# Grouping weight products into two runs instead of three, with row sums in the output bank, in an attention + ReGLU kernel on one core

## Chip, cores, metric

One core of one Trainium2 chip. The metric is device time in microseconds (us) of one execution. Executions of one kernel in one series lie 0.2 to 2.1 us apart; each kernel is told with the median and the lowest and highest of its fast runs (no timed run was in the slow state; single executions have no state).

## The reference, cut to what matters

```python
# x [8, 8, 512, 64], state [8, 8, 32, 64]: batches, heads, rows, width
a  = softmax(x @ state.T / 8);  xread = a @ state
a2 = softmax(state @ x.T / 8);  sread = a2 @ x
y  = concat([xread, sread])              # per batch 512 + 32 rows, 8 heads x 64 = 512 columns
out = (relu(y @ w_gate) * (y @ w_val)) @ w_out     # 512 -> 1536 -> 512
```

## The kernel before

The kernel never forms `xread`. Per batch it multiplies the small state by the gate and value weights ("weight products", `up`, kept in `U`, bf16), and then `gv` multiplies `U` by the normalised scores. `gv` goes in 12 slices of 128 columns of the 1536; after each slice TensorE (PE) runs a piece of an earlier batch's output product (`out_piece`). One thing more is hung into certain slices: scores, weight products, and row sums (`sr`) for the second softmax. These are the parts that matter:

```python
def bank(name, kind="r"):            # PSUM has 8 banks: 0 to 5 rotate, 6 and 7 are for output pieces
    ...
    n = turn["r"] % 6 if kind == "r" else 6 + turn["o"] % 2
    turn[kind] += 1
...
def u_unit(b, w, lo):                # one weight-product unit: 8 matmuls of 64x32 tiles, 512 columns
    ps = held["u", b, w, lo] = [bank("up"), bank("up")]        # two banks
    u_mm(ps, b, w, lo, 512)
...
def u_block(b, lo, engs=("act", "act", "dve", "dve")):         # a run: two units, four casts out of PSUM
    for w in range(2):
        u_unit(b, w, lo)
        for kc in range(NK):
            u_out(b, w, lo, kc, engs[2 * w + kc])

def att_half(b, kc):                 # scores, exp (ScalarE), then sums and scaling on VectorE
    att_up(b, kc)
    ...
first, lag = 2 * NF + 4, 18
at(2, 4, x_dma, 4, (nc.sync,))
for b in range(3, B):
    s, late = b - 1, 2 if b == 3 else 0        # batch b's work is hung into the slices of batch b-1
    for i, jf in enumerate((3, 5)):
        at(s, jf + late, att_half, b, i)
    for i, jf in enumerate((7, 9, 11)):
        at(s, jf, u_block, b, 512 * i)
    ...
for g in range(first, NF * (B + 1)):
    b, jf = divmod(g, NF)
    gv(b, jf) if b < B else gvs(jf)
    relu(b, jf)                      # ScalarE, reads the first bank of gv
    mult(b, jf)                      # VectorE: h = value * relu(gate), reads the second bank
    if g >= lag:
        out_piece(*divmod(g - lag, NF))
    for f in units.get(g, ()):       # what was hung in with at(...)
        f()
```

Each engine runs its instructions in the order in which the program emits them. "Batch 2's slices" are those of `gv(2, ...)`; batch 3's scores and weight products are in them. The scheduled part that is discussed starts at slice 4 of batch 2; a hand-made program before it is the same in both kernels.

The softmax here doesn't subtract the row's maximum and nothing guards it: scores larger than these inputs give would overflow.

Of the kernel before, what the change touches and what calls it, by code (L numbers as in the profile page):

```python
# [16 lines left out]
def kernel(  # L17
# [9 lines left out]
    nc = tc.nc  # L27

    B, H, S, D = x.shape
# [5 lines left out]
    NF = d_ff // 128  # L35
# [19 lines left out]
    NK = 2  # L55
# [7 lines left out]
    NX, DP = 2, 66  # L63
# [15 lines left out]
    given, turn = [], {"r": 0, "o": 0}  # L79

    def bank(name, kind="r"):

        if given:
            n = given.pop(0)
        else:
            n = turn["r"] % 6 if kind == "r" else 6 + turn["o"] % 2
            turn[kind] += 1
        return psum.tile([128, 512], FP32, name=name, tag=f"b{n}")

    held = {}  # L90
# [33 lines left out]
    def state_T(g):  # L124
        ps = held["st", g] = bank("stT_ps").bitcast(BF16)[:, 0:512]
        for i in range(4):
            nc.tensor.transpose(ps.rearrange("p (q i m) -> p q i m", i=4, m=8)[:, :, i],
                                st_b[:, g % 3, i].rearrange("p h d -> p (h d)"), id128)
# [31 lines left out]
    def x_T(b, j):  # L160

        if b not in xT:
            xT_alloc(b)
        ps = bank("xT_ps").bitcast(BF16)[:, 0:512].rearrange("p (c t) -> p c t", c=NC)
        for c in range(NC):
            if b == 0 and j < 2:
                nc.tensor.transpose(ps[:, c], x_head(b)[:, c, 2 * j:2 * j + 2].rearrange("p h d -> p (h d)"), id128)
            else:
                v, h = (x_tail(b), 2 * j - HK) if b == 0 else (xb[b], 2 * j)
                for h2 in range(2):  # L170
                    nc.tensor.transpose(ps[64 * h2:64 * h2 + 64, c], v[:, c, h + h2], id128)
        held["xT", b, j] = ps
# [4 lines left out]
    def x_T2(b, half):  # L177
        if b not in xT:
            xT_alloc(b)
        ps = held["xT2", b, half] = bank("xT_ps").bitcast(BF16).rearrange("p (c j t) -> p c j t", c=NC, j=2)  # L180
        for j in range(2):
            for c in range(NC):
                for h2 in range(2):
                    nc.tensor.transpose(ps[64 * h2:64 * h2 + 64, c, j], xb[b][:, c, 4 * half + 2 * j + h2], id128)  # L184
# [68 lines left out]
            src = src.rearrange("p c h d -> p h c d")  # L253
            nc.gpsimd.tensor_copy(out=v[:, hs:hs + src.shape[1]], in_=src)  # L254

    def sr_mm(b):

        ps = held["sr", b] = bank("sr_ps")[:, 0:2 * DP].rearrange("p (r d) -> p r d", r=2)
        for c in range(NC):
            for parity in range(2):  # L260
                for j in range(NJ):
                    nc.tensor.matmul(ps[32 * j:32 * j + 32, parity, 0:D + 1], e_sn[b][:, parity, c, 32 * j:32 * j + 32],  # L262
                                     xa[:, b % NX, H * c + 2 * j + parity, 0:D + 1],
                                     start=(c == 0 and parity == 0), stop=(c == NC - 1), skip_group_check=True)

    def sr_norm(b):
        ps = held["sr", b]
        rr = small.tile([128, 2], FP32, name="rr", tag="rr")
        nc.vector.reciprocal(out=rr, in_=ps[:, :, D])
        sn = held["sn", b] = small.tile([128, 2, D], BF16, name="sn", tag="sn")  # L270
        nc.vector.tensor_tensor(out=sn, in0=ps[:, :, 0:D], in1=rr.to_broadcast([128, 2, D]), op=ALU.mult)
# [20 lines left out]
    def u_unit(b, w, lo):  # L292

        u_alloc(b)
        ps = held["u", b, w, lo] = [bank("up"), bank("up")]
        u_mm(ps, b, w, lo, 512)

    def u_out(b, w, lo, kc, eng):
        copy[eng](out=U[b][:, w, kc, lo:lo + 512], in_=held["u", b, w, lo][kc])  # L299
# [17 lines left out]
    def gv(b, jf):  # L317
        if b not in hsb:
            hsb[b] = hpool.tile([128, NF, S], BF16, name="h_sb", tag="h_sb")
        held["gv", b, jf] = [bank("gv_ps"), bank("gv_ps")], hsb[b][:, jf], S  # L320
        for w in range(2):
            for kc in range(NK):
                gv_mm(held["gv", b, jf][0], b, jf, w, kc)

    def gvs(jf):
        f0 = jf * 128
        ps = [bank("gv_ps"), bank("gv_ps")]
        nt = B * Ns
        for w, wsb in ((0, wg_sb), (1, wv_sb)):
            for j in range(NJ):  # L330
                nc.tensor.matmul(ps[w][:, 0:nt], wsb[:, j, f0:f0 + 128], br[:, j].rearrange("p b n -> p (b n)"),  # L331
                                 start=(j == 0), stop=(j == NJ - 1))
        held["gv", B, jf] = ps, hs_sb[:, jf], nt

    def relu(b, jf):
        ps, dst, n = held["gv", b, jf]
        g_sb = held["g", b, jf] = gpool.tile([128, 512], BF16, name="g_sb", tag="g_sb")
        nc.scalar.activation(out=g_sb[:, 0:n], in_=ps[0][:, 0:n], func=AF.Relu)  # L338

    def mult(b, jf):  # L340
        ps, dst, n = held["gv", b, jf]
        nc.vector.tensor_tensor(out=dst, in0=ps[1][:, 0:n], in1=held["g", b, jf][:, 0:n], op=ALU.mult)  # L342
# [4 lines left out]
    def out_mms(src, b, tsub, jfs):  # L347
        if jfs[0] == 0:
            held["o", b, tsub] = o_bank()
        for jf in jfs:  # L350
            nc.tensor.matmul(held["o", b, tsub], src[:, jf, tsub * 128:(tsub + 1) * 128], wo_sb[:, jf],  # L351
                             start=(jf == 0), stop=(jf == NF - 1))
# [4 lines left out]
    def fin_x(b, tsub, eng="act"):  # L357
        o_sb = opool.tile([128, d_model], FP32, name="o_sb", tag="o_sb")
        copy[eng](out=o_sb, in_=held["o", b, tsub])  # L359
        nc.sync.dma_start(out=out_rows(b, tsub), in_=o_sb)  # L360

    def fin_s(t2):
        outr = out.rearrange("(b s) m -> b s m", s=SP)
        o_sb = opool.tile([128, d_model], FP32, name="o_sb", tag="o_sb")
        nc.scalar.copy(out=o_sb, in_=held["o", B, t2])
        for bq in range(4):
            eng = nc.sync if bq % 2 == 0 else nc.scalar
            eng.dma_start(out=outr[t2 * 4 + bq, S:SP], in_=o_sb[bq * Ns:(bq + 1) * Ns])
# [14 lines left out]
    def out_part(b, i):  # L383
        tsub, q = divmod(i, 3)
        out_mms(hsb[b], b, tsub, list(range(4 * q, 4 * q + 4)))

    def out_piece(b, i):
        out_part(b, i)
        if i % 3 == 2:
            fin_x(b, i // 3)  # L390
# [37 lines left out]
    def spin(n, cols=512):  # L428
        for i in range(n):
# [6 lines left out]
             "sc": att_sc, "ex": att_exp, "nr": att_sum, "nx": att_scale, "aT2": att_T2, "ao2": att_out2, "aT": att_T, "ao": att_out,  # L436
             "c": c_unit, "co": c_out, "u": u_unit, "uo": u_out, "gv": gv, "re": relu, "mu": mult, "o": out_part,
             "of": fin_x, "xn": x_next, "xp": x_pad, "sr": sr_mm, "sn": sr_norm}
    program = """
    dx.1.0.2 dx.1.1.2 stc.0.0.act stc.0.1.dve spin.7 stT.0@0 xc.0.0.dve dw.0.0.128 sto.0.act dw.1.0.128 on xc.0.1.dve  # L440
# [31 lines left out]
        assert not given  # L472


    units = {}

    def at(b, jf, f, *args):
        units.setdefault(NF * b + jf, []).append(lambda: f(*args))

    def u_block(b, lo, engs=("act", "act", "dve", "dve")):  # L480
        for w in range(2):
            u_unit(b, w, lo)
            for kc in range(NK):
                u_out(b, w, lo, kc, engs[2 * w + kc])

    def att_half(b, kc):
        att_up(b, kc)
# [7 lines left out]
        att_scale(b, kc)  # L495

    def sr(b):
        sr_mm(b)
        sr_norm(b)

    def state_prep(lo, hi):
# [2 lines left out]
            state_out(g, "act")  # L504

    first, lag = 2 * NF + 4, 18
    at(2, 4, x_dma, 4, (nc.sync,))
    at(2, 10, state_prep, 4, B)
    for b in range(3, B):
        s, late = b - 1, 2 if b == 3 else 0  # L510
        for i, jf in enumerate((3, 5)):
            at(s, jf + late, att_half, b, i)
        for i, jf in enumerate((7, 9, 11)):
            at(s, jf, u_block, b, 512 * i)
        if b + 1 < B:
            at(s, 9, x_next, b + 1)
            at(s, 9, x_pad, b + 1)
        if b + 2 < B:
            at(s, 10, x_dma, b + 2, (nc.sync,))
    for b in range(B):  # L520
        s, jf = {0: (2, 2), 1: (2, 3), 2: (2, 8), 3: (2, 11)}.get(b, (b - 1, 9))
        if b > 1:
            at(s, jf, sr, b)
        at(*divmod(NF * s + jf + 2, NF), sr_T, b, "act")
    for g in range(first, NF * (B + 1)):
        b, jf = divmod(g, NF)
        gv(b, jf) if b < B else gvs(jf)
        relu(b, jf)
        mult(b, jf)
        if g >= lag:  # L530
            out_piece(*divmod(g - lag, NF))
        for f in units.get(g, ()):
            f()
    for t2 in range(2):
        out_mms(hs_sb, B, t2, list(range(NF)))
        fin_s(t2)
# [33 lines left out]
```

## Time and profile before

226.34 us (226.18 to 226.71, 3 runs); the profiled execution spans 224.4 us.

| | before |
|---|---|
| PE busy | 98% |
| VectorE / ScalarE / GpSimd busy | 57% / 56% / 24% |
| chain of waits that ended last | 91% PE |
| gv slice or output piece | 0.865 us, start to start |
| a batch in the steady part | 23.76 us |

From the page of the kernel before: the busy table, the clock granted to PE by slice (tenths), and the chain of waits by engine.

```profile
PE 219.3 (98%) x1967; PEld 104.8 (47%) x1967; DVE 128.6 (57%) x226; ACT 124.8 (56%) x236; POOL 53.0 (24%) x58
...
PEclk9999999999999999999999999999999999999999
...
PE 91%; DMA 4%; POOL 3%; issue 0%; DVE 0%; POOLq 0%; DVEq 0%
```

PE has almost no time off, so the busy share says nothing about where it loses. For that the timeline of PE is better read by differences of starts. The columns are start, time taken, engine, line, operation, output and inputs, tile, shape and count; matmuls overlap, so the times taken add to more than the time that passes. This is the kernel before in batch 4's slices 7 to 11 and on:

```profile
111.17 1.03 PE L351 MATMUL o_ps<-wo_sb,h_sb 128*128 128x512 bf16 x4
112.13 0.41 PE L289 MATMUL up<-wg_sb,stT 64*32 64x512 bf16 x8
112.36 0.40 PE L289 MATMUL up<-wv_sb,stT 64*32 64x512 bf16 x8
112.69 1.04 PE L314 MATMUL gv_ps<-ans,U 128*128 128x512 bf16 x4
...
120.95 0.40 PE L289 MATMUL up<-wv_sb,stT 64*32 64x512 bf16 x8
121.28 0.23 PE L275 MATMUL srT_ps<-id,sn 128*128 128x128 bf16 x1
121.35 1.20 PE L314 MATMUL gv_ps<-ans,U 128*128 128x512 bf16 x4
122.38 1.02 PE L351 MATMUL o_ps<-wo_sb,h_sb 128*128 128x512 bf16 x4
```

The piece at 111.17 has the array for 0.865 us, to 112.035. The first unit starts at 112.13, 0.095 late; the second 0.23 later; `gv` follows the second by 0.33 where a further unit would follow by 0.23. So this run pays about 0.10 us to enter and 0.10 to leave. Units use the array in tiles of 64x32, `gv` and the pieces use it whole (128*128 in the lines); entering and leaving are changes of that mode. At 121.35 `gv` holds the array until 122.38, 1.03 us instead of 0.865.

### The profile page before, as it was taken

How to read it: one execution, taken by the hardware profiler on the slowest of the kernel's cores; microseconds unless marked ns; L12 is line 12 of the kernel's file. 1: busy time of each engine (PE TensorE's matmuls, PEld its weight loads, DVE VectorE, ACT ScalarE, POOL GpSimd, SP SyncE). 2: the span in 40 equal slices, each digit the busy share in tenths (PEclk: the TensorE clock that was granted, in tenths of full speed). 3: DMA queues.
4: the chain of work that ended last, by engine and by line, in shares of the span. 5: the costliest groups of instructions: out<-in, count | busy, mean ns of one | idle time of the engine just before them, and what ended most of it. 6: DMA issues, size and time to landing. Idle time of an engine off the chain costs nothing.

```text
span 224.4 us, 4871 instructions
## 1 busy us (share of the span) xinstructions
PE 219.3 (98%) x1967; PEld 104.8 (47%) x1967; DVE 128.6 (57%) x226; ACT 124.8 (56%) x236; POOL 53.0 (24%) x58
## 2 busy tenths in 40 slices
PE   7999999999999999999999999999999999999994
PEld 3544454444444444434444443445444445666543
DVE  3687788576486667754866477646865433222100
ACT  4699877773666655664466455655546444322221
POOL 8798756412352150015000600000000000000000
PEclk9999999999999999999999999999999999999999
DMA  6999999160809612681159213511311111112132
GB/s 155 177 195 197 209 231 282 41 167 0 250 34 197 227 48 80 144 246 51 48 124 261 84 47 78 112 50 47 93 50 47 48 47 50 48 58 75 58 94 93
DMA packets 37799, 25.48 MB, mean 114 GB/s; under 512 B 18864, under 2 KB 33200, under 8 KB 37776
## 3 DMA queue, kind: packets, MB, share of 16 engines
q1 hardware_dynamic: 24912, 16.85, 26.6%
q0 software_dynamic: 11968, 7.47, 21.5%
q10 hardware_dynamic: 896, 0.85, 1.3%
q8 instruction: 15, 0.25, 0.5%
q14 instruction: 8, 0.07, 0.1%
HBM read 18.35 MB, written 8.91 MB: 121 GB/s over the span
## 4 chain that ended last, share of the span: by engine, by line
PE 91%; DMA 4%; POOL 3%; issue 0%; DVE 0%; POOLq 0%; DVEq 0%
PE o_ps L351 38%; PE gv_ps L314 37%; PE gv_ps L331 5%; PE up L289 4%; DMA wv_sb<-in_moe_w_val_dram 4%; PE upc L289 1%; PE sr_ps L262 1%; PE sc_ps L198 1%; PE o_ps L377 1%; POOL wg_sb L108 1%; POOL xb L418 1%; POOL wv_sb L108 1%; PE xT_ps L184 0%; PE aT_ps L233 0%; POOL xb L410 0%; PE srT_ps L275 0%
## 5 line engine op out<-in xcount | busy, mean ns | idle before, releaser
L314 PE MATMUL gv_ps<-ans,U 128*128 128x512 bf16 x384 | 96.7, 380 | 0.1
L351 PE MATMUL o_ps<-wo_sb,h_sb 128*128 128x512 bf16 x372 | 94.6, 379 | 0.0
L338 ACT ACTIVATE g_sb<-gv_ps 128x512 bf16<-128x512 f32 (+1 forms) x108 | 63.1, 584 | 47.0 <-PE gv_ps L314 32.5
L342 DVE TENSOR_TENSOR h_sb<-gv_ps,g_sb 128x512 bf16<-128x512 f32 x96 | 65.3, 688 | 41.8 <-ACT g_sb L338 40.5
L351 PEld LDWEIGHTS <-h_sb 128*128 128x128 bf16 x372 | 36.0, 98 | 41.0 <-issue 0.7
L314 PEld LDWEIGHTS <-U 128*128 128x128 bf16 x384 | 34.8, 98 | 41.4 <-issue 4.2
L359 ACT COPY o_sb<-o_ps 128x512 f32<-128x512 f32 x29 | 17.0, 585 | 20.7 <-PE o_ps L351 20.7
L299 DVE CAST U<-up 128x512 bf16<-128x512 f32 x36 | 23.2, 685 | 5.3 <-PE up L289 5.2
L299 ACT CAST U<-up 128x512 bf16<-128x512 f32 x36 | 19.4, 592 | 10.1 <-PE up L289 10.1
L140 POOL CAST xb<-xf 128x1024 bf16<-128x1024 f32 x10 | 10.4, 1066 | 53.2 <-DMA xf<-in_x_dram 53.2
L254 POOL COPY xa<-xb 128x2048 bf16<-128x2048 bf16 (+1 forms) x9 | 15.3, 1710 | 13.8 <-issue 7.0
L211 DVE TENSOR_REDUCE cs<-e_sn 128x16 f32<-128x512 bf16 x16 | 10.9, 684 | 8.6 <-ACT e_sn L205 8.6
L342 DVE TENSOR_TENSOR hs_sb<-gv_ps,g_sb 128x256 bf16<-128x256 f32 x12 | 5.1, 425 | 15.4 <-PE gv_ps L331 10.5
L205 ACT ACTIVATE e_sn<-sc_ps 128x512 bf16<-128x512 f32 x16 | 9.6, 600 | 5.6 <-PE sc_ps L198 5.5
L309 ACT CAST U<-upc 128x512 bf16<-128x512 f32 (+1 forms) x20 | 9.7, 532 | 1.4 <-PE upc L289 1.3
L289 PEld LDWEIGHTS <-stT 64*32 64x32 bf16 x512 | 5.0, 89 | 11.2 <-issue 10.9
L430 PE MATMUL warm_ps<-hs_sb 128*128 128x512 bf16 x23 | 7.8, 456 | 1.2 <-DVE hs_sb L394 1.2
L217 DVE TENSOR_TENSOR a_sn<-e_sn,rc 128x512 bf16<-128x512 bf16 x12 | 8.3, 692 | 0.6
L198 PEld LDWEIGHTS <-xT 128*128 128x128 bf16 x128 | 5.7, 98 | 3.8 <-ACT xT L175 0.7
L331 PE MATMUL gv_ps<-br,wg_sb 128*128 128x256 bf16 x48 | 7.2, 273 | 0.0
L331 PE MATMUL gv_ps<-br,wv_sb 128*128 128x256 bf16 x48 | 7.2, 273 | 0.0
L289 PE MATMUL up<-wg_sb,stT 64*32 64x512 bf16 x144 | 7.2, 386 | 0.0
(64 smaller groups left out, 129.0 us busy)
## 6 DMA issues: line engine op xcount, KB each, us to landing
out_dram<-o_sb SPq DMA_DIRECT2D x31, 256.0 KB, 2.3
xf<-in_x_dram SPq DMA_DIRECT2D x4, 1024.0 KB, 6.5
wo_sb<-in_moe_w_out_dram POOLq DMA_DIRECT2D x2, 768.0 KB, 14.5
wg_sb<-in_moe_w_gate_dram POOLq DMA_DIRECT2D x5, 256.0 KB, 8.8
wv_sb<-in_moe_w_val_dram POOLq DMA_DIRECT2D x5, 256.0 KB, 9.4
xf<-in_x_dram POOLq DMA_DIRECT2D x1, 1024.0 KB, 15.2
xb<-in_x_dram POOLq DMA_DIRECT2D x3, 256.0 KB, 6.3
xb<-in_x_dram POOLq DMA_DIRECT2D x1, 512.0 KB, 11.6
```

What stands on the lines that cost most here:

```text
L140: copy[eng](out=xb[b][:, :, hs].rearrange("p c h d -> p h c d"), in_=xf[b][:, hs])
L211: nc.vector.reduce_sum(out=cs, in_=e_v, axis=AX.X)
L254: nc.gpsimd.tensor_copy(out=v[:, hs:hs + src.shape[1]], in_=src)
L289: nc.tensor.matmul(dst[parity][32 * j:32 * j + 32], stT[r:r + 64, b, j, 32 * parity:32 * parity + 32], wsb[r:r + 64, j, lo:lo + n], start= ...
L299: copy[eng](out=U[b][:, w, kc, lo:lo + 512], in_=held["u", b, w, lo][kc])
L309: copy[eng](out=U[b][:, :, kc, lo:lo + n], in_=held["c", b, lo][kc])
L314: nc.tensor.matmul(ps[w], U[b][:, w, kc, f0:f0 + 128], ANS[b][:, kc].rearrange("p c t -> p (c t)"), start=(kc == 0), stop=(kc == NK - 1))
L331: nc.tensor.matmul(ps[w][:, 0:nt], wsb[:, j, f0:f0 + 128], br[:, j].rearrange("p b n -> p (b n)"), start=(j == 0), stop=(j == NJ - 1))
L338: nc.scalar.activation(out=g_sb[:, 0:n], in_=ps[0][:, 0:n], func=AF.Relu)
L342: nc.vector.tensor_tensor(out=dst, in0=ps[1][:, 0:n], in1=held["g", b, jf][:, 0:n], op=ALU.mult)
L351: nc.tensor.matmul(held["o", b, tsub], src[:, jf, tsub * 128:(tsub + 1) * 128], wo_sb[:, jf], start=(jf == 0), stop=(jf == NF - 1))
L359: copy[eng](out=o_sb, in_=held["o", b, tsub])
```

## The change

Three things. The six units of a batch form two runs of three units (slices 7 and 10) instead of three runs of two. Three units take all six rotating banks, so the next output piece is run early, right behind the run, to give ScalarE and VectorE time to empty banks. And the row sums take the output bank that is idle at that time. Around it, batch 3's scores move from slices 5 and 7 to 4 and 6, batch 4's load from slice 4 to 6, the preparation of the later states (`state_prep`) from 10 to 8, row sums of batches 2 and 3 to slices 7 and 10 and later ones to 10, and later transposes to one slice behind their sums.

```diff
+        elif kind == "spare":
+            n = 6 + turn["o"] % 2
...
-    def u_block(b, lo, engs=("act", "act", "dve", "dve")):
-        for w in range(2):
+    def u_block(b, part):
+        for w, lo in ((0, 0), (1, 0), (0, 512), (1, 512), (0, 1024), (1, 1024))[3 * part:3 * part + 3]:
             u_unit(b, w, lo)
-            for kc in range(NK):
-                u_out(b, w, lo, kc, engs[2 * w + kc])
+            u_out(b, w, lo, 0, "act")
+            u_out(b, w, lo, 1, "dve")
...
     def sr(b):
-        sr_mm(b)
+        sr_mm(b, "spare")
...
-    at(2, 4, x_dma, 4, (nc.sync,))
-    at(2, 10, state_prep, 4, B)
+    at(2, 6, x_dma, 4, (nc.sync,))
+    at(2, 8, state_prep, 4, B)
     for b in range(3, B):
-        s, late = b - 1, 2 if b == 3 else 0
+        s, late = b - 1, 1 if b == 3 else 0
         for i, jf in enumerate((3, 5)):
             at(s, jf + late, att_half, b, i)
-        for i, jf in enumerate((7, 9, 11)):
-            at(s, jf, u_block, b, 512 * i)
+        for part, jf in enumerate((7, 10)):
+            at(s, jf, u_block, b, part)
+            paired.add(NF * s + jf)
...
-        s, jf = {0: (2, 2), 1: (2, 3), 2: (2, 8), 3: (2, 11)}.get(b, (b - 1, 9))
+        s, jf = {0: (2, 3), 1: (2, 4), 2: (2, 7), 3: (2, 10)}.get(b, (b - 1, 10))
...
-        at(*divmod(NF * s + jf + 2, NF), sr_T, b, "act")
+        at(s, jf + (2 if b in (2, 3) else 1), sr_T, b, "act")
...
         for f in units.get(g, ()):
             f()
+        if g in paired:
+            out_piece(*divmod(piece, NF))
+            piece += 1
```

More of the change, by code (lines that the diff above doesn't have):

```diff
@@ L254, in x_pad, with sr_mm @@
             nc.gpsimd.tensor_copy(out=v[:, hs:hs + src.shape[1]], in_=src)
-    def sr_mm(b):
-        ps = held["sr", b] = bank("sr_ps")[:, 0:2 * DP].rearrange("p (r d) -> p r d", r=2)
+    def sr_mm(b, kind="r"):
+        ps = held["sr", b] = bank("sr_ps", kind)[:, 0:2 * DP].rearrange("p (r d) -> p r d", r=2)
         for c in range(NC):
@@ L472 @@
         assert not given
-    units = {}
+    units, paired = {}, set()
     def at(b, jf, f, *args):
         units.setdefault(NF * b + jf, []).append(lambda: f(*args))
-    def u_block(b, lo, engs=("act", "act", "dve", "dve")):
-        for w in range(2):
+    def u_block(b, part):
+        for w, lo in ((0, 0), (1, 0), (0, 512), (1, 512), (0, 1024), (1, 1024))[3 * part:3 * part + 3]:
             u_unit(b, w, lo)
-            for kc in range(NK):
-                u_out(b, w, lo, kc, engs[2 * w + kc])
+            u_out(b, w, lo, 0, "act")
+            u_out(b, w, lo, 1, "dve")
     def att_half(b, kc):
@@ L520 @@
     for b in range(B):
-        s, jf = {0: (2, 2), 1: (2, 3), 2: (2, 8), 3: (2, 11)}.get(b, (b - 1, 9))
+        s, jf = {0: (2, 3), 1: (2, 4), 2: (2, 7), 3: (2, 10)}.get(b, (b - 1, 10))
         if b > 1:
             at(s, jf, sr, b)
-        at(*divmod(NF * s + jf + 2, NF), sr_T, b, "act")
+        at(s, jf + (2 if b in (2, 3) else 1), sr_T, b, "act")
+    piece = first - lag
     for g in range(first, NF * (B + 1)):
@@ L529 @@
         mult(b, jf)
-        if g >= lag:
-            out_piece(*divmod(g - lag, NF))
+        if piece <= g - lag:
+            out_piece(*divmod(piece, NF))
+            piece += 1
         for f in units.get(g, ()):
             f()
+        if g in paired:
+            out_piece(*divmod(piece, NF))
+            piece += 1
     for t2 in range(2):
```

## The prediction

> **What bounds it now.** The page's busy table has TensorE (PE) busy 98% of the span, at full granted clock in every slice; the chain of waits is 91% PE. The PE timeline from 74 to 189 us is one unbroken stream: a gv slice (4 matmuls 128x512) and an out piece (4) take 0.865 us each, start to start. Only what PE does between these counts. VectorE (57%) and ScalarE (56%) have slack.
>
> **What PE pays now per batch (97.58 to 121.35 = 23.77 us).** 24 groups x 0.865 = 20.76; two score units 0.46; the rest, 2.55, is weight-product ("up") runs, sums and a transpose:
> - run at slice 7: due at 112.04, starts 112.13; second unit 0.23 later, next gv 0.33 after that. So 0.65, of which two units are 0.45; entering costs 0.095, leaving 0.105.
> - run at 9 with row sums: 115.29+0.865 to 117.17 = 1.02.
> - run at 11 and transpose: 0.65+0.07; then gv takes 1.03 until the out piece instead of 0.865: 0.17 lost (121.35 to 122.38, in four batches). Its second half needs the bank that ScalarE still evicts: cast from 121.31 to about 121.85, the matmul's weight load at 121.95.
>
> The Trainium skill, "TensorEngine Tiling (Array Packing)", Key Properties, says that changing the tiling mode drains the engine; up is 64x32, row sums 128x32, gv 128x128, and the trace agrees: 0.10 us at each change.
>
> **What the change does.** Same matmuls, evictions and bytes. It removes one of three runs per batch: -0.20 us. With the run at slice 11 goes the bank wait: -0.17. Row sums still follow an up run: no change. In batch 2's slices, sums of batches 2 and 3 and three runs make four runs (63.8, 66.2, 68.4, 73.0); they become two, with one more inner change of mode: -0.30.
>
> Added: six casts per run take all six rotating banks. An estimate from the trace's durations (T = the run's start): casts start at T+0.48, VectorE's three (0.61 apart, 0.69) end at T+2.4, ScalarE's at T+2.1. The early piece holds PE until T+1.65 at slice 7 and T+2.0 at 10; gv then needs the first unit's banks, free at T+1.2: no wait. The third unit needs the banks of the gv before, whose product ends about T+0.13, before T+0.45. Tightest is the row-sum transpose, now one slice after the sums: reciprocal and product (0.16, 0.29) queue behind three casts and end about T+2.78; PE reaches the transpose at T+2.88, its weights are needed 0.1 before. So 0 to 0.15 us lost, in four batches. The idle output bank is next wanted over 2 us later: no wait.
>
> **On the critical path: all of it**, since PE streams to the end. 4 x (0.20+0.17-0.07) + 0.30 = 1.5 us saved.
>
> **Predicted: 224.8 us, 8 in 10 between 224.1 and 225.9; faster by over 2%: 0.01, within 2%: 0.97, slower: 0.02.**
>
> **What would show it.** Batch period 23.4 to 23.55 us; two up runs per batch with three units 0.23 apart; entering and leaving still 0.10 each; no gv over 0.90 after the transpose; transpose weights waiting for VectorE by 0.15 at most; PE busy down 1 to 2 us, other engines' totals unchanged.
>
> **What would make it wrong.** Casts slower than in pairs, so that gv, relu or transpose waits several tenths per run; the out copy behind three ScalarE casts delaying relu until banks run out; gv slices 8 and 9 back to back catching a bank unevicted; batch 3's scores, one slice earlier, waiting for input; a cost of mode changes that goes with units, not runs.

## The result, and the profile after

225.78 us (225.37 to 226.03, 4 runs) against 226.26 us (225.94 to 226.71) in the same rounds: ratio 0.9975, 95% interval 0.9951 to 1.0. A ratio here is the mean time of one kernel's runs over that of the other's in the same rounds, so not quite the ratio of the medians quoted. A third of the forecast saving of 1.5 us arrived. Six runs more (after_again, below) gave 0.9971.

The page after, same lines:

```profile
PE 216.0 (96%) x1937; PEld 106.5 (48%) x1967; DVE 128.9 (57%) x226; ACT 124.9 (56%) x236; POOL 52.8 (24%) x58
...
PEclk9999999999999999999999999999999999999999
...
PE 94%; issue 2%; ACT 2%; DVE 1%; DVEq 0%
```

PE is busy 3.3 us less, but the span is 0.2 us shorter, so PE now stands idle somewhere. (Part of the 3.3 is records missing from this trace, 1937 of 1967 matmuls: often the first output matmul after a run, where the timeline then shows "x3" and 0.16 us of "issue". That is no wait.) The steady part, batch 4's slices 7 to 11 in the changed kernel:

```profile
112.00 1.03 PE L353 MATMUL o_ps<-wo_sb,h_sb 128*128 128x512 bf16 x4
112.96 0.41 PE L291 MATMUL up<-wg_sb,stT 64*32 64x512 bf16 x8
113.18 0.40 PE L291 MATMUL up<-wv_sb,stT 64*32 64x512 bf16 x8
113.40 0.45 PE L291 MATMUL up<-wg_sb,stT 64*32 64x512 bf16 x8
...
119.84 0.43 PE L264 MATMUL sr_ps<-xa,e_sn 128*32 128x65 bf16 x32
...
121.08 1.03 PE L316 MATMUL gv_ps<-ans,U 128*128 128x512 bf16 x4
121.94 0.22 PE L277 MATMUL srT_ps<-id,sn 128*128 128x128 bf16 x1
122.00 1.03 PE L316 MATMUL gv_ps<-ans,U 128*128 128x512 bf16 x4
122.86 0.81 PE L353 MATMUL o_ps<-wo_sb,h_sb 128*128 128x512 bf16 x3
```

Two runs of three, units 0.22 to 0.23 apart, a change of mode still 0.10, and `gv` at 122.00 takes 0.86. Row sums follow each other at 23.42 us a batch (before 23.76). That is the forecast, at its better end. Now batch 2's slices. Before, slice 7 and the `gv` of slice 8:

```profile
63.81 0.41 PE L289 MATMUL up<-wg_sb,stT 64*32 64x512 bf16 x8
64.03 0.40 PE L289 MATMUL up<-wv_sb,stT 64*32 64x512 bf16 x8
64.36 1.04 PE L314 MATMUL gv_ps<-ans,U 128*128 128x512 bf16 x4
```

and after, at slice 7:

```profile
64.61 0.40 PE L291 MATMUL up<-wv_sb,stT 64*32 64x512 bf16 x8
64.83 0.38 PE L291 MATMUL up<-wg_sb,stT 64*32 64x512 bf16 x1
65.75 0.41 PE L291 MATMUL up<-wg_sb,stT 64*32 64x512 bf16 x7 [0.55 <-DVE h_sb L344]
66.09 0.43 PE L264 MATMUL sr_ps<-xa,e_sn 128*32 128x65 bf16 x32
```

The third unit starts one of its eight matmuls at 64.83 and the other seven at 65.75: it waited for `h_sb`, VectorE's product, as that frees the second bank of the `gv` before. PE then reached the row sums at 66.09 instead of 64.83+0.33, 0.93 us late. VectorE in that stretch:

```profile
62.14 0.69 DVE L344 TENSOR_TENSOR h_sb<-gv_ps,g_sb 128x512 bf16<-128x512 f32 x1
63.40 0.69 DVE L213 TENSOR_REDUCE cs<-e_sn 128x16 f32<-128x512 bf16 x1 [0.56 <-ACT e_sn L207]
...
64.41 0.69 DVE L219 TENSOR_TENSOR a_sn<-e_sn,rc 128x512 bf16<-128x512 bf16 x1
65.02 0.68 DVE L344 TENSOR_TENSOR h_sb<-gv_ps,g_sb 128x512 bf16<-128x512 f32 x1
```

Between the product of slice 6 (62.14) and that of slice 7 (65.02) VectorE waits for the exponential and then does the sums, reciprocal and scaling of batch 3's second score half. In the program order they stand between the two products.

To compare executions without the start, I take the time from the row sums of batch 1 (the last common point ahead of the changed slices) to the first product of the summed states (behind the last batch), and call it the body. Before: 133.91 us. After: 133.12. Of the difference of -0.79, the four later batches give 4 x (23.42-23.76) = -1.4, and so batch 2's slices cost +0.6, where the forecast had -0.3.

The start differed too: those row sums began at 55.85 us before, 56.44 after, in code that is the same. The warming matmuls at 4.4 us, before and then after:

```profile
4.40 0.81 PE L430 MATMUL warm_ps<-hs_sb 128*128 128x512 bf16 x3
```

```profile
4.56 1.49 PE L432 MATMUL warm_ps<-hs_sb 128*128 128x512 bf16 x3
```

Three took 0.81 us in one and 1.49 in the other, after seven of them in about 3 us in both. By their starts, the seven follow each other by 0.43 us in both; the three then by 0.21 before, but still by 0.43 after, where the step to 0.21 comes only at about 6.7 us. The Trainium skill, "TensorE: Matmul & The Clock Gate", Part 1, says that the array's clock rises after an activity window that runs freely, so that the moment varies by about 500 ns either way from run to run. A spacing that halves fits such a clock, but the size does not fit: over the profiles kept here, with the first of these matmuls at 1.17 or 1.18 us in each, the step comes by 4.2 us in one and at 6.7 in another, at least 2.5 us apart. The profile's own clock column reads full speed there, so the clock itself is not shown.

### The profile page after: what moved, and what is told of

It reads as the page before. It is cut to its first block, busy times and chain, and to the rows that moved or that the text cites. A ratio compares the mean times of both kernels' runs of the same rounds, so it can differ in the third digit from the quotient of the medians.

```text
span 224.2 us, 4840 instructions
## 1 busy us (share of the span) xinstructions
PE 216.0 (96%) x1937; PEld 106.5 (48%) x1967; DVE 128.9 (57%) x226; ACT 124.9 (56%) x236; POOL 52.8 (24%) x58
## 4 chain that ended last, share of the span: by engine, by line
PE 94%; issue 2%; ACT 2%; DVE 1%; DVEq 0%
PE o_ps L353 37%; PE gv_ps L316 36%; PE gv_ps L333 5%; PE up L291 4%; PE warm_ps L432 3%; PE sc_ps L200 2%; PE upc L291 1%; PE sr_ps L264 1%; PE o_ps L379 1%; ACT U L311 1%; PE aT_ps L235 1%; PE xT_ps L186 1%; ACT e_sn L207 0%; PE stT_ps L129 0%; ACT xT L189 0%
## 5 line engine op out<-in xcount | busy, mean ns | idle before, releaser
L316 PE MATMUL gv_ps<-ans,U 128*128 128x512 bf16 x373 | 93.9, 379 | 0.5
L353 PE MATMUL o_ps<-wo_sb,h_sb 128*128 128x512 bf16 x357 | 91.6, 379 | 2.1 <-issue 1.9
L316 PEld LDWEIGHTS <-U 128*128 128x128 bf16 x384 | 35.7, 98 | 40.3 <-issue 0.6
L353 PEld LDWEIGHTS <-h_sb 128*128 128x128 bf16 x372 | 35.2, 98 | 39.9 <-issue 1.7
L291 PEld LDWEIGHTS <-stT 64*32 64x32 bf16 x512 | 5.7, 89 | 12.1 <-issue 11.0
L291 PE MATMUL up<-wg_sb,stT 64*32 64x512 bf16 x144 | 7.7, 382 | 0.5 <-DVE h_sb L344 0.5
```

The costliest lines, as they stand in the source:

```text
L291: nc.tensor.matmul(dst[parity][32 * j:32 * j + 32], stT[r:r + 64, b, j, 32 * parity:32 * parity + 32], wsb[r:r + 64, j, lo:lo + n], start= ...
L316: nc.tensor.matmul(ps[w], U[b][:, w, kc, f0:f0 + 128], ANS[b][:, kc].rearrange("p c t -> p (c t)"), start=(kc == 0), stop=(kc == NK - 1))
L353: nc.tensor.matmul(held["o", b, tsub], src[:, jf, tsub * 128:(tsub + 1) * 128], wo_sb[:, jf], start=(jf == 0), stop=(jf == NF - 1))
```

## The experiments

All ran on the chip and gave right results. "Body" is as above, from one profile.

| run | median us (range) | ratio to before, 95% | body us | batch us |
|---|---|---|---|---|
| before (its profile) | 226.34 (226.18 to 226.71) | 1 | 133.91 | 23.76 |
| changed | 225.78 (225.37 to 226.03) | 0.9975 (0.9951 to 1.0) | 133.12 | 23.42 |
| after_again | 226.19 (225.12 to 227.03) | 0.9971 (0.9947 to 0.9995) | 133.13 | 23.42 |
| sums_at_8 | 225.65 (224.74 to 226.78) | 0.9956 (0.9924 to 0.9988) | 132.91 | 23.42 |
| scores_4_5 | 224.87 (224.55 to 225.19) | 0.9916 (0.9899 to 0.9932) | 132.28 | 23.42 |
| before_T_later | 226.49 (225.81 to 227.2) | 0.9987 (0.9963 to 1.0011) | 133.70 | 23.59 |
| scores_4_6_all | 229.5 (229.33 to 229.53) | 1.0105 (1.0065 to 1.0144) | 136.62 | 24.29 |
| six_runs | 229.69 (229.28 to 229.94) | 1.0113 (1.0072 to 1.0154) | 136.77 | 24.28 |
| no_early | 226.65 (226.22 to 227.33) | 0.9984 (0.9941 to 1.0027) | 134.19 | 23.68 |
| sums_rotating | 227.51 (227.28 to 227.94) | 1.0025 (0.9977 to 1.0073) | 134.82 | 23.75 |
| x_early | 224.86 (224.5 to 225.2) | 0.9912 (0.9888 to 0.9937) | 132.28 | 23.42 |
| x_early_scores_2_4 | 224.63 (224.35 to 224.75) | 0.9899 (0.9872 to 0.9925) | 132.04 | 23.36 |
| x4_at_4 | 226.33 (225.66 to 226.84) | 0.9973 (0.9948 to 0.9997) | 133.36 | 23.42 |
| loads_at_8 | 225.93 (225.34 to 226.78) | 0.9962 (0.9939 to 0.9985) | 133.12 | 23.42 |

The theory: the steady saving is real, and VectorE's place in the order of batch 2's slices gave two thirds of it back through the bank. The rivals: the change costs something in every run; ScalarE or the three-unit run itself makes the halt; the start is delayed by the change.

### The changed kernel again

No edit.

> The changed kernel once more, for a tighter interval and a second profile. Segment theory: the profile after the first was 0.6 us late already at the first steady slice (row sums of batch 1 at 56.44 instead of 55.85 us), in code that the change does not touch, because three warming matmuls ran slowly at 4.6 us; that is chance and differs by execution. Then from that slice to the end the kernel takes 0.8 us less than before (1.38 saved in batches 3 to 7, 0.59 lost in batch 2's slices) in this profile too, and the timed ratio is about 0.9965 (0.9955 to 0.9975). Rival, that the change itself delays the start: the row sums of batch 1 start at 56.4 us again, ratio 0.9990 to 1.0.

Row sums of batch 1 began at 55.54 us this time and the body was 133.13: the changed code does not delay the start. Ratio as expected.

### Sums behind slice 8's product

```diff
-            at(s, jf + late, att_half, b, i)
+            if b == 3 and i == 1:
+                at(s, 6, att_sc, b, i)
+                at(s, 6, att_exp, b, i)
+                at(s, 8, att_sum, b, i)
+                at(s, 8, att_scale, b, i)
+                at(s, 8, att_aT_dma, b)
+            else:
+                at(s, jf + late, att_half, b, i)
```

> PE's order is unchanged; only VectorE's sums and scaling of batch 3's second score half are put behind the product of slice 8 instead of behind that of slice 6. Theory (VectorE has 1.7 us of sums and scaling between the products of slices 6 and 7, so the bank that the third unit needs is freed late): the 0.93 us halt inside the run at slice 7 of batch 2 goes, 0.9 us less than after_again, ratio to before about 0.9925. Rival (ScalarE's exponentials or the three-unit run itself hold it): the halt stays over 0.4 us.

The orders of PE and ScalarE are the same, only VectorE's differs (and the transfer that follows its scaling). In batch 2's slices:

```profile
64.10 0.40 PE L291 MATMUL up<-wg_sb,stT 64*32 64x512 bf16 x8
64.43 0.43 PE L264 MATMUL sr_ps<-xa,e_sn 128*32 128x65 bf16 x32
```

The halt is gone entirely; row sums of batch 1 to those of batch 3 took 15.65 us instead of 16.58, the 0.93. So VectorE's order was the cause. But the median fell by 0.5 us only, and the body in its profile by 0.2. The profile shows a new halt one batch later, from GpSimd (POOL) and VectorE (DVE):

```profile
82.61 1.89 POOL L256 COPY xa<-xb 128x2048 bf16<-128x2048 bf16 x1
82.63 2.41 DVE L219 TENSOR_TENSOR a_sn<-e_sn,rc 128x512 bf16<-128x512 bf16 x1
```

GpSimd's copy of batch 5's x started 0.02 us before VectorE's scaling of batch 4's scores, and the scaling took 2.41 us instead of 0.69. The product of slice 7 came late again, and PE lost 0.71 us in that run, at its second and third units (row sums of batch 3 to batch 4: 24.13 us instead of 23.42). The Trainium skill, "SBUF — State Buffer", Who interferes with whom, says that VectorE and GpSimd share one pair of ports as an exclusive lock, that a VectorE instruction with two inputs in SBUF needs it while GpSimd reads SBUF, and that whoever issues first blocks the other. The scaling has two SBUF inputs, and this trace agrees: the copy took its usual 1.89 us, and the scaling ended 0.54 us after it. The kernel before has a near tie of the same kind. There VectorE was first in one profile, and GpSimd took 2.29 us for two casts that otherwise take 2.02:

```profile
62.20 0.69 DVE L217 TENSOR_TENSOR a_sn<-e_sn,rc 128x512 bf16<-128x512 bf16 x1
...
62.49 2.29 POOL L140 CAST xb<-xf 128x1024 bf16<-128x1024 f32 x2 [4.15 <-DMA xf<-in_x_dram]
```

and in another execution of the same slices (profile of before_T_later, which differs only from batch 3's slices on) GpSimd was first, and the scaling took 1.41:

```profile
62.32 2.48 POOL L140 CAST xb<-xf 128x1024 bf16<-128x1024 f32 x2 [3.68 <-DMA xf<-in_x_dram]
62.50 1.41 DVE L217 TENSOR_TENSOR a_sn<-e_sn,rc 128x512 bf16<-128x512 bf16 x1
```

PE then lost about 0.5 us there (row sums of batch 1 to batch 3: 18.19 us instead of 17.71). Some executions of the kernel before pay for that and others don't; how many is not known.

### Batch 3's scores at slices 4 and 5

```diff
-        for i, jf in enumerate((3, 5)):
-            at(s, jf + late, att_half, b, i)
+        for i, jf in enumerate((4, 5) if b == 3 else (3, 5)):
+            at(s, jf, att_half, b, i)
```

> Batch 3's second score half one slice earlier (4 and 5 instead of 4 and 6), the spacing to the run at 7 as in the later batches. VectorE theory: halt at the third unit 0 to 0.2 us instead of 0.93; 0.75 to 0.9 us less than after_again, ratio to before about 0.993. Rival as above: halt stays over 0.4 us.

```profile
64.18 0.47 PE L291 MATMUL up<-wg_sb,stT 64*32 64x512 bf16 x8
64.58 0.43 PE L264 MATMUL sr_ps<-xa,e_sn 128*32 128x65 bf16 x32
```

From the third unit to the row sums 0.40 us instead of 1.26 (0.33 without any wait). The body fell by 0.84 us and the median by 1.3 under after_again's, its neighbour on that chip; ratio 0.9916, slightly better than expected. The other 0.5 us of the median is not explained by the bodies. This is faster than both kernels, by under 1%. In this profile one scaling met a cast and took 1.58 us, without a halt.

### The kernel before, transpose one slice later

```diff
-        at(*divmod(NF * s + jf + 2, NF), sr_T, b, "act")
+        at(*divmod(NF * s + jf + (3 if b > 3 else 2), NF), sr_T, b, "act")
```

> The kernel before with the transpose of the row sums of batches 4 to 7 one slice later (slice 0 of the next batch in place of 11). Nothing else. Theory: the 0.17 us that gv lost after it came from the rotation of the banks (its second half got the bank that ScalarE was still evicting); with the transpose elsewhere gv gets the two banks of the gv before and the loss goes: 4 x 0.17 = 0.7 us less than before, ratio 0.997, no gv at slice 0 over 0.90 us. Rival (the loss belongs to leaving the 64x32 mode through a transpose, or to fresh weights): it stays or moves, ratio 1.000.

The `gv` after the run at slice 11 now holds the array 0.88 us (121.88 to 122.76) instead of 1.03, and each batch takes 23.59 instead of 23.76 us: the 0.17 us went with the transpose. By itself that does not exclude the rival, that the loss comes from leaving the units' mode through a transpose, as the transpose no longer follows a unit here. The profile of six_runs (below) excludes it: there the transpose still follows a unit, whose run is shorter and takes fewer banks, and `gv` behind it holds the array 0.86 us, to the piece at 124.40. So the 0.17 us was the bank.

```profile
123.47 0.23 PE L275 MATMUL srT_ps<-id,sn 128*128 128x128 bf16 x1
123.54 1.03 PE L314 MATMUL gv_ps<-ans,U 128*128 128x512 bf16 x4
```

The timed ratio, 0.9987, neither shows nor excludes the 0.7 us: its interval holds both 0.997 and 1.0. The body fell by only 0.2, as in this profile the near tie told above cost about 0.5.

### Scores at 4 and 6 in every batch

```diff
-        s, late = b - 1, 1 if b == 3 else 0
+        s, late = b - 1, 1
```

> The changed kernel with the second half of the scores at slice 6 (4 and 6) in every batch, as batch 3 has it, instead of 3 and 5 in the later ones. VectorE theory: the halt of 0.6 to 0.95 us at the third unit of the run at slice 7 appears in batches 4 to 7 too: 2.4 to 3.8 us slower than the changed kernel, ratio to before 1.007 to 1.013. Rival (something of batch 2's slices alone): no new halt, ratio 0.9965.

The halt came in all four later batches as well, and the body grew by 3.50 us:

```profile
114.11 0.38 PE L291 MATMUL up<-wg_sb,stT 64*32 64x512 bf16 x1
115.03 0.41 PE L291 MATMUL up<-wg_sb,stT 64*32 64x512 bf16 x7 [0.55 <-DVE h_sb L344]
```

The rival "batch 2 alone" falls.

### Six runs of one unit

```diff
-    def u_block(b, lo, engs=("act", "act", "dve", "dve")):
-        for w in range(2):
-            u_unit(b, w, lo)
-            for kc in range(NK):
-                u_out(b, w, lo, kc, engs[2 * w + kc])
+    def u_block(b, w, lo):
+        u_unit(b, w, lo)
+        u_out(b, w, lo, 0, "act")
+        u_out(b, w, lo, 1, "dve")
...
-        for i, jf in enumerate((7, 9, 11)):
-            at(s, jf, u_block, b, 512 * i)
+        for i in range(6):
+            at(s, 6 + i, u_block, b, i % 2, 512 * (i // 2))
```

> The kernel before with the six units of weight products as six runs of one unit (slices 6 to 11) instead of three of two. Theory, a cost of 0.20 us per run for entering and leaving the mode: 15 more runs, +3.0 us, less 0.7 us as the bank wait after the transpose goes with the shorter run: +2.3 us, ratio 1.010. Rival, a cost that goes with the units: ratio about 0.997.

```profile
110.95 1.03 PE L351 MATMUL o_ps<-wo_sb,h_sb 128*128 128x512 bf16 x4
111.91 0.41 PE L289 MATMUL up<-wg_sb,stT 64*32 64x512 bf16 x8
112.25 1.04 PE L314 MATMUL gv_ps<-ans,U 128*128 128x512 bf16 x4
```

From the piece to `gv` 1.30 us: 0.865 for the piece, 0.225 for the unit, 0.21 for the two changes of mode. A batch takes 0.52 us more than before: three more runs at 0.21, less the bank wait of 0.17, make 0.46. The cost goes with the runs.

### No early piece

```diff
-            paired.add(NF * s + jf)
```

> The changed kernel without the piece run early: gv of the next slice follows the run at once. Theory: its first bank is free 1.1 us after the run's start, PE arrives after 0.8 us at slice 7 and 1.15 us at slice 10: a halt of about 0.3 us at slice 7, 0 to 0.1 at slice 10, in five batches: 1.5 to 2 us slower than the changed kernel, ratio to before about 1.004. Rival (the early piece buys nothing): ratio as the changed kernel, 0.9965.

```profile
113.31 0.45 PE L291 MATMUL up<-wg_sb,stT 64*32 64x512 bf16 x8
113.98 1.02 PE L316 MATMUL gv_ps<-ans,U 128*128 128x512 bf16 x4 [0.21 <-ACT U L301]
```

`gv` waits for ScalarE's cast: 0.67 us after the third unit instead of 0.33, at slice 7. At slice 10 the row sums fill that time and nothing is lost. A batch takes 0.26 us more, the body 1.07, below the 1.5 to 2 expected: in batch 2's slices the long halt covers it, and the changed kernel's third unit already loses 0.07 at slice 7. The timed interval is too wide to add to this.

### Row sums in a rotating bank

```diff
-        sr_mm(b, "spare")
+        sr_mm(b)
```

> The changed kernel with the row sums back in the rotating banks. Theory: they are the seventh bank after six and wait for the first unit's eviction, free 1.1 us after the run's start while PE arrives at 0.78: a halt of 0.3 to 0.4 us in each of the six row sums, 1.8 to 2.2 us slower than the changed kernel, ratio to before about 1.005. Rival (which bank does not matter): ratio 0.9965.

```profile
119.73 0.40 PE L291 MATMUL up<-wv_sb,stT 64*32 64x512 bf16 x8
120.40 0.43 PE L264 MATMUL sr_ps<-xa,e_sn 128*32 128x65 bf16 x32 [0.27 <-ACT U L301]
```

The row sums wait 0.34 us for the first unit's cast in five of the six places (in the sixth the halt comes first), and the body grows by 1.70 us, to 0.9 more than before. So, by the bodies, the idle output bank is needed for the change to pay at all; the timed interval holds 1.0.

### Earlier loads of x, on scores_4_5

```diff
-    at(2, 6, x_dma, 4, (nc.sync,))
+    at(2, 5, x_dma, 4, (nc.sync,))
...
-            at(s, 10, x_dma, b + 2, (nc.sync,))
+            at(s, 8, x_dma, b + 2, (nc.sync,))
```

> scores_4_5 with the loads of x issued earlier (batch 4's at slice 5 instead of 6, later ones at slice 8 instead of 10), so that GpSimd's casts and copies of x end well before VectorE's scaling of the next scores. Theory of the shared port: the scaling (two inputs in SBUF) took 0.69 us everywhere except where a GpSimd copy had started first, there 1.41 to 2.41 us; in scores_4_5 one of ten took 1.58. Here all ten take 0.69; as that one did not stop PE, the median moves little (224.4 to 225.0 us, ratio 0.991), with executions at most 0.6 us apart. Rival (chance): some scaling is long again.

All ten scalings took 0.69 us in its profile; body and median are those of scores_4_5. As expected it buys room, not time.

### Scores at 2 and 4 in the later batches, on x_early

```diff
-        for i, jf in enumerate((4, 5) if b == 3 else (3, 5)):
+        for i, jf in enumerate((4, 5) if b == 3 else (2, 4)):
```

> x_early with the score halves of batches 4 to 7 at slices 2 and 4 instead of 3 and 5. Theory: in the changed kernel the third unit at slice 7 still waits 0.07 us for the product of slice 7, which follows that of slice 6 back to back behind the second scaling; one slice more clears that: period of a batch 23.35 instead of 23.42 us, 0.3 us in four batches, ratio to before about 0.990. Rival (the 0.07 us belongs to leaving the run): period stays 23.42.

A batch takes 23.36 us, and the body is 0.24 us shorter: the last 0.06 us at the third unit was the same wait on VectorE. This is the fastest version, 224.63 us, ratio 0.9899. That it is faster than x_early rests on the profiles; the timed intervals overlap.

### Batch 4's load at slice 4 in the changed kernel

```diff
-    at(2, 6, x_dma, 4, (nc.sync,))
+    at(2, 4, x_dma, 4, (nc.sync,))
```

> The changed kernel with the load of batch 4's x back at slice 4, where the kernel before has it. Theory of the shared port: GpSimd's casts then run from about 62.4 to 64.5 us and meet the second scaling of batch 3's scores (63.5 us): it takes 1 to 1.7 us instead of 0.69 and the halt of the third unit grows from 0.93 us by the same: 0.3 to 1 us slower than the changed kernel, ratio to before about 0.999 to 1.001. Rival (GpSimd does not matter): scaling 0.69, halt 0.93, ratio 0.997.

The second scaling took 0.92 us, and the body 0.24 more. The direction is the theory's, the size below it: GpSimd was near the end of its second cast when the scaling came. The ratio is the changed kernel's, as an effect this small does not show in the times.

### The loads alone moved, in the changed kernel

```diff
-            at(s, 10, x_dma, b + 2, (nc.sync,))
+            at(s, 8, x_dma, b + 2, (nc.sync,))
```

> The changed kernel, only the loads of x for batches 5 to 7 issued at slice 8 instead of 10; the halt at the third unit of batch 2's slices (0.93 us) is left in. Theory: the changed kernel's executions spread over 225.1 to 227.0 us because in some of them GpSimd's copy of batch 5's x has started when VectorE scales batch 4's first scores (in one profile 2.41 us instead of 0.69, and 0.72 us of PE time lost), and in the profiled ones it ended only 0.4 us before. With the copy over by 78 us that can't happen: executions within 0.8 us of each other, median 0.3 to 0.8 us under the changed kernel's, ratio to before 0.9930 to 0.9960. Rival (the spread is the start-up's chance): spread and median as the changed kernel, ratio 0.997.

A miss. The body is the changed kernel's 133.12 and the times spread by 1.4 us. So I could not hold that GpSimd spreads the changed kernel's times.

### Four more looks at the changed kernel

> The changed kernel unaltered, for one more profile of an execution (one of four). Theory: beyond the start-up (row sums of batch 1 anywhere from 55.5 to 56.5 us), executions differ in batches 2 and 3: either the halt at batch 2's third unit is longer than 0.93 us or one of VectorE's scalings in batch 3's slices meets GpSimd's copy and takes over 1 us, with a halt of up to 0.7 us at that run's third unit. Rival: in all four the halt is 0.93 us, all ten scalings are 0.69 us, and only the start-up differs.

> As after_look1, the second of four profiles: either a longer halt or a long scaling in batches 2 and 3 in some of them, or none and only the start-up differs.

> As after_look1, the third of four profiles: either a longer halt or a long scaling in batches 2 and 3 in some of them, or none and only the start-up differs.

> As after_look1, the fourth of four profiles: either a longer halt or a long scaling in batches 2 and 3 in some of them, or none and only the start-up differs.

225.54, 225.67, 225.65 and 226.0 us, with one run of the kernel before on that chip at 226.85. The bodies are 133.12, 133.11, 133.13 and 133.12, all scalings 0.69, the halt the same. The row sums of batch 1 began at 55.93, 56.09, 56.06 and 56.42. The rival holds for what was profiled: from there on the kernel ran the same each time, and in the six profiles of it only the start varied, by 0.9 us. But the longest execution among these six took 226.03 us, and four of the six timed in after_again took 226.07 to 227.03; no profile shows what lengthened those. In the latest, after_look4, the three warming matmuls took 1.49 us, as in the first profile; but after_look3, where they took 0.81, began at 56.06 and not at 55.54, so that warming is not the whole of it.

## Why the prediction was right or wrong

- **What bounds it: right.** Every halt of PE in the body came out as body time: 0.93 removed gave 0.93 (sums_at_8, batch 1 to 3).
- **Cost by run, 0.20 us: right.** six_runs measured 0.21 for each further run.
- **Bank wait of 0.17 us: right.** Moving the transpose alone removed it (23.76 to 23.59), and so did a shorter run with the transpose left behind it (six_runs).
- **Steady batches, 23.4 to 23.55 us: right**, 23.42. The transpose of the sums, which I had feared to lose up to 0.15 us, lost nothing: `gv` at 121.08 is followed by it at 121.94, 0.86 later. The third unit at slice 7 lost 0.07 instead. The forecast had taken off 0.07 for the transpose; that the two misses are of one size, so that the sum came out nearly right, is luck.
- **Batch 2's slices, "-0.30": wrong.** They cost about 0.6 us more than before. The step that failed is "The third unit needs the banks of the gv before, whose product ends about T+0.13, before T+0.45". I worked that out from the timing of a slice that has no scores before it, and applied it to all five batches. T+0.13 is what the kernel before shows at slice 11 (run at 120.72, product ended at 120.85); at slice 7 it shows T+0.43 even in the steady part (112.13 and 112.56), as the changed kernel does (112.96 and 113.39), which is the 0.07 above. In batch 2's slices the second score half is in slice 6, one slice before the run, and not two as in the others; VectorE's sums and scaling stood ahead of the product, which ended at 65.70, T+1.31. The banks themselves were named rightly, and "batch 3's scores, one slice earlier" stood among the risks, but as a wait for their input, not as work in front of VectorE's product. sums_at_8 and scores_4_5 took the halt away, and scores_4_6_all put it into every batch.
- **The total.** With that step mended, in scores_4_5, the body is 1.63 us below the kernel before's, and the forecast saving was 1.5. The median of 225.78 lay in the range given, at its slow edge, but that says little, as the range ended only 0.4 us under the kernel before; the saving was a third of the one forecast: -1.4 and +0.6 make -0.8 in the body. The medians show 0.5 of these 0.8. The difference is within the interval of the timing, and the start, which varies by 0.9 us, is large enough for it; it was not taken apart further. (The 0.8 is against the profile of before in which VectorE was first; an execution where GpSimd is first has a longer body there.)
- **"PE busy down 1 to 2 us": not decided**, as 30 matmul records are missing behind the 3.3 us that the page shows. **"Other engines' totals unchanged": right**, VectorE 128.6 and 128.9, ScalarE 124.8 and 124.9 us.

## What to carry to other kernels

When a group of instructions is made longer until it uses every bank, find for each bank who reads it last and what stands in front of that reader in its engine's order, separately in each place where the group occurs; the odd place, here batch 3, the first of the five, is the one to check. Price a regrouping by the number of mode changes, and give the engine that empties the banks a piece of independent work to hide behind: without the early piece 1.1 us were lost, without the idle bank 1.7, of 1.4 saved in the steady batches. Where run times vary by more than the effect, measure from a common point in the traces: the same kernel's body came out equal within 0.02 us in six executions whose starts differed by 0.9.

## What the Trainium skill lacked or had wrong

- "TensorEngine Tiling (Array Packing)", Key Properties: it says that a change of tiling mode drains the engine, but not what that costs. Here 0.10 us to enter tiles of 64x32 from 128x128 and 0.10 to leave them for 128x128 or 128x32, 0.21 for a run in and out.
- "TensorE: Matmul & The Clock Gate", Back-to-back issue gap: it gives about 131 ns for each 128x512 matmul in a sustained stream with weight loads, and calls 216 ns the isolated gap. Here, in a stream with a new weight load for each matmul, four took 0.865 us, 216 ns each.
- "SBUF — State Buffer", Who interferes with whom: the rule held; the section gives no times for VectorE instructions with two SBUF inputs. Here 0.69 us grew to 1.41 and 2.41 when GpSimd was first, and GpSimd's 2.02 for two casts to 2.29 when VectorE was.
- "TensorE: Matmul & The Clock Gate", Part 1: it has the moment at which the array speeds up vary by about 500 ns either way, though it also says that the number of slow matmuls differs from run to run; here the spacing of the matmuls halved at moments at least 2.5 us apart (by 4.2 us in one profile, at 6.7 in another), and the profile's clock column showed nothing of it. It puts the penalty of the warm-up at under 1% of a typical span. Starts differed by 0.9 us of 224 here, not by the warm-up alone; that is under 1% too, but more than this change saved, so it has to be taken out of a comparison.
